# Queueing loads and output transposes behind the next transpose of the row maximum, in an attention and two-layer MoE kernel

## The chip, the cores and the metric

The kernel runs on one core of a Trainium2 chip. The metric is device time of one execution in microseconds. Three executions of the kernel before took 803.95, 791.01 and 797.76 us; the median is 797.76 us.

## The reference, cut to what matters

Sixteen heads (2 batches of 8) of clustered attention, then two pairs of dense layers on the joined heads:

```python
q_n, k_n, c_n = (x / (norm(x) + 1e-6) for x in (q, k, centroids))
mask   = argmax(q_n @ c_n.T) == argmax(k_n @ c_n.T)      # 16 clusters
scores = where(mask, q @ k.T / sqrt(64), -1e9)           # 768 x 768 per head
attn   = exp(scores - max(scores)); attn /= sum(attn) + 1e-9
x      = (attn @ v), heads joined: 1536 x 512
x      = softplus(x @ w_in)  @ w_out                     # 512 -> 2048 -> 512
out    = leaky (x @ w_in2) @ w_out2                      # 512 -> 2048 -> 512
```

The inputs are float32, the weights come as 64-bit floats.

## The kernel before

**Attention, one head at a time.** Everything is kept as pairs of 16-bit halves. For head h, `split` (L188) makes halves of q and k and has them transposed by a DMA (tile `t`, L197). `assign_mm` and `assign_el` (L200 to L234) find the cluster of each row: 24 small matmuls and five VectorE operations, L219 to L225. The one-hot clusters go beside q and k into the tiles `nq` and `nk`, which two more DMA transposes (`tq`, L232; `tk`, L233) turn. `emit_s1` (L239) makes the scores a first time, 12 matmuls of 384 columns (L244), and takes each half row's maximum on VectorE (L251, tile `mm`). `emit_m` (L253) folds them into one maximum per row (L256), writes it into `nq` and has `nq` transposed once more: the tile `tm` (L259). Only then can `emit_s2` (L262) make the scores a second time with the maximum subtracted inside the matmul (L277, and L278, which reads `tm`), ScalarE takes the exponential (L284), GpSimd its low half (L286), and `emit_pv` (L291) multiplies by v (L300, L313, L314, L318). `emit_empty` (L333, matmuls L336) ends the head, `emit_norm` (L338) divides and, after each second head, transposes the joined result into the MoE's input by two DMAs (`xth`, `xtl`, L360). v itself is loaded by `load_v` (L177, DMA L180) two heads ahead and split by `split_v` (L183).

**Weights.** A weight matrix arrives in pieces of 512 KB, 16 per matrix, through two staging tiles `st` (DMA L134). `conv` turns a piece into two half-precision tiles: three integer operations on VectorE (L142, L145, L148), one copy on ScalarE (L152), and one subtraction on VectorE (L153). A staging tile is free again after L148. `w_step` (L516) traces the conversion of the last piece and the load of the next one. Pieces are counted here from 0: 0 to 15 are w_in, 16 to 31 w_out, 32 to 47 the second w_in and 48 to 63 the second w_out. The last 32 go into memory that the attention's tiles hold until its end.

**MoE.** The tokens go in four blocks of 384. `layer_in` has 16 steps of 12 matmuls (L415), each followed by an activation (L383 and L384 on ScalarE, L385 on VectorE; block 0 has another form, L393 to L398); `layer_mid` has 4 outputs of 48 matmuls (L428), which are evacuated by L432 and L433; the second pair is L415 again and `layer_out` (L447, output L453). Steps of block 0 are traced among heads 8 to 15.

**What sets the order.** All DMAs are issued by SyncE (SP), in one order, and an issue that waits holds up all behind it. Every engine executes its instructions in the order that a list scheduler made when the program was built: it takes what is ready by a priority (`at_pri`; a lower number is earlier, a head is one unit) in a timeline of its own. So an edge that is added at one place moves instructions elsewhere too. `tc.issue_after(x)` adds such an edge: what is traced in the block stands behind instruction x on x's own engine. PSUM has eight banks: two rings `s1` and `s2` of two banks for scores, one each for `as` and `x`, and `m0` and `m1` for weights and MoE. In heads 0 to 7 the ring `s2` takes `m1` as a third bank.

## Time and profile before

| | before |
|---|---|
| median of three runs | 797.76 us |
| the profiled execution, its own time | 799.24 us |
| its span, first to last instruction | 797.5 us |
| TensorE busy in the span | 732.4 us, 92% |
| VectorE, ScalarE, GpSimd busy | 389.3, 318.6, 189.2 us |
| mean granted TensorE clock | 0.949 of full speed |
| transposes of the maximum (`tm`), issue to landing | 2.5 to 4.7 us, median 2.8 us, 16 of them |

The page's first part gives busy time by engine, its second the busy tenths of forty equal slices of the span (19.9 us each) with the clock that TensorE was granted. Times are microseconds from the span's start. SP, the queue that issues DMAs, is never counted as busy; its waits are in a view of their own. A busy TensorE can be a slow one: at half clock a matmul takes twice as long and is busy all the while, so busy time is read beside the granted clock.

### The profile page before, as it was taken

The page shows a single profiled execution, that of the slowest core. Times are in us where ns is not written, and L with a number is a line of the kernel's source. Part 1 is how long each engine was busy: PE and PEld are TensorE (multiplying, and loading weights), DVE is VectorE, ACT ScalarE, POOL GpSimd, SP SyncE. Part 2 cuts the span into 40 slices and gives each one's busy share as a digit, 9 for nine tenths or more (in the row PEclk, how much of TensorE's full clock was granted, in tenths as well). Part 3 has the DMA queues.
Part 4 walks back from the last instruction along what each step waited for, and adds up shares of the span by engine and source line. Part 5 has one row for each costly group of instructions (what it writes and reads, how often), then busy time and mean ns, then how long its engine had stood idle before and what let it go on. Part 6 is the DMA issues. An engine that isn't in the chain of part 4 may idle for free.

```text
span 797.5 us, 14209 instructions
## 1 busy us (share of the span) xinstructions
PE 732.4 (92%) x5808; PEld 439.6 (55%) x5808; DVE 389.3 (49%) x819; ACT 318.6 (40%) x739; POOL 189.2 (24%) x176
## 2 busy tenths in 40 slices
PE   1589989889889898899998999999999999999998
PEld 1167757545556565566564566666545645645643
DVE  4876767588798888328788902201201200200210
ACT  5366655537766646135224503303402402411410
POOL 4256655437766747200000000000000000000000
PEclk9988978669899899999999999999999999999999
DMA  8986444684854655214455300000000000000000
GB/s 196 228 173 129 103 106 109 159 156 130 167 143 130 131 105 134 80 21 131 151 168 163 129 1 1 1 1 0 1 14 27 1 14 26 2 14 27 1 14 26
DMA packets 104881, 66.03 MB, mean 83 GB/s; under 512 B 90992, under 2 KB 95088, under 8 KB 104816
## 3 DMA queue, kind: packets, MB, share of 16 engines
q1 hardware_dynamic: 104816, 65.13, 33.5%
q8 instruction: 45, 0.74, 0.4%
q14 instruction: 20, 0.16, 0.1%
HBM read 43.02 MB, written 3.15 MB: 58 GB/s over the span
## 4 chain that ended last, share of the span: by engine, by line
PE 65%; DMA 16%; DVE 12%; ACT 3%; issue 2%; SPq 1%; POOL 0%; ACTq 0%; DVEq 0%
PE m L415 23%; PE m L447 16%; PE m L428 11%; DMA tm<-nq 4%; DMA st<-in_moe_w_in_dram 4%; DMA st<-in_moe_w_out_dram 3%; PE s L278 3%; PE s L244 3%; PE s L277 2%; DMA t<-n 2%; DVE mm L251 2%; PE x L300 2%; DVE wc L148 2%; DVE wc L145 2%; DMA tk<-nk 1%
## 5 line engine op out<-in xcount | busy, mean ns | idle before, releaser
L385 DVE TENSOR_TENSOR g_l<-mr,g_h 128x384 f16<-128x384 f32 x112 | 62.3, 557 | 208.4 <-ACT mr L384 208.4
L286 POOL TENSOR_TENSOR pl<-p 128x768 f16<-128x768 f32 x80 | 117.4, 1474 | 84.2 <-ACT p L284 70.2
L251 DVE TENSOR_REDUCE mm<-s 128x1 f32<-128x384 f32 x192 | 102.4, 552 | 30.7 <-PE s L244 29.7
L415 PE MATMUL m<-xth,w_inh 128*128 128x384 f16 x256 | 86.5, 339 | 4.8 <-DVE xtl L433 3.9
L383 ACT ACTIVATE g_h<-m 128x384 f16<-128x384 f32 x112 | 54.6, 488 | 89.5 <-PE m L415 89.5
L428 PE MATMUL m<-g_h,w_outh 128*128 128x384 f16 x256 | 83.5, 326 | 4.4 <-DVE w_outl L153 2.6
L415 PE MATMUL m<-xtl,w_inh 128*128 128x384 f16 x256 | 86.4, 338 | 0.0
L428 PE MATMUL m<-g_l,w_outh 128*128 128x384 f16 x256 | 83.4, 326 | 2.3 <-DVE g_l L385 2.2
L428 PE MATMUL m<-g_h,w_outl 128*128 128x384 f16 x256 | 83.3, 326 | 0.0
L415 PE MATMUL m<-xth,w_in2h 128*128 128x384 f16 x256 | 83.3, 326 | 0.0
L415 PE MATMUL m<-xtl,w_in2h 128*128 128x384 f16 x256 | 83.3, 326 | 0.0
L284 ACT ACTIVATE p<-s 128x384 f32<-128x384 f32 x144 | 67.4, 492 | 31.1 <-PE s L278 28.6
L244 PE MATMUL s<-tk,tq 80*128 80x384 f16 x192 | 68.7, 381 | 12.1 <-DVE mm L251 7.9
L415 PEld LDWEIGHTS <-w_inh 128*128 128x128 f16 x512 | 51.4, 101 | 41.0 <-issue 10.6
L447 PE MATMUL m<-w_out2h,g_h 128*128 128x512 f16 x192 | 72.8, 379 | 0.0
L447 PE MATMUL m<-w_out2l,g_h 128*128 128x512 f16 x192 | 72.8, 379 | 0.0
L447 PE MATMUL m<-w_out2h,g_l 128*128 128x512 f16 x192 | 72.8, 379 | 0.0
L428 PEld LDWEIGHTS <-w_outh 128*128 128x128 f16 x512 | 49.6, 98 | 37.8 <-issue 3.2
L415 PEld LDWEIGHTS <-w_in2h 128*128 128x128 f16 x512 | 50.1, 98 | 33.4
L278 PE MATMUL s<-tm,tk 81*128 81x384 f16 x160 | 57.2, 374 | 11.9 <-DMA tm<-nq 11.4
L447 PEld LDWEIGHTS <-g_h 128*128 128x128 f16 x384 | 37.6, 98 | 44.9
L277 PE MATMUL s<-t 128*128 128x384 f16 x160 | 57.0, 360 | 5.1 <-ACT p L284 4.2
(108 smaller groups left out, 1224.5 us busy)
## 6 DMA issues: line engine op xcount, KB each, us to landing
st<-in_moe_w_in_dram SPq DMA_DIRECT2D x32, 512.0 KB, 4.2
st<-in_moe_w_out_dram SPq DMA_DIRECT2D x32, 512.0 KB, 3.5
qk<-in_q_dram SPq DMA_DIRECT2D x16, 192.0 KB, 3.2
qk<-in_k_dram SPq DMA_DIRECT2D x16, 192.0 KB, 3.3
v<-in_v_dram SPq DMA_DIRECT2D x16, 192.0 KB, 3.1
out_dram<-ob SPq DMA_DIRECT2D x12, 256.0 KB, 2.0
t<-n SPq DMA_TRANSPOSE x16, 4.1
tq<-nq SPq DMA_TRANSPOSE x16, 4.3
```

The lines of the kernel that those rows point to most:

```text
L145: V.scalar_tensor_tensor(out=c, in0=hi, scalar=-0x40000000, in1=c, op0=ALU.bitwise_and, op1=ALU.bitwise_or)
L244: PE.matmul(out=o, lhsT=t[0:KS1, c, :], rhs=tk[0:KS1, 3 * j:3 * j + 3, :], start=True, stop=True,)
L251: V.reduce_max(out=mms[h % 2][:, c, j:j + 1], in_=bank[:, 0:3 * 128], axis=AX)
L277: PE.matmul(out=o, lhsT=t1[:, kt, 1, :], rhs=t1[:, 3 * j:3 * j + 3, 0, :], start=True, stop=False)
L278: PE.matmul(out=o, lhsT=t2[0:KS2, kt, :], rhs=tqh[0:KS2, 3 * j:3 * j + 3, :], start=False, stop=True)
L284: S.activation(out=p[:, j, :], in_=sp, func=AF.Exp, scale=scale)
L286: G.tensor_tensor(out=pl, in0=p, in1=pb, op=ALU.subtract)
L383: S.activation(out=late["h"][:, m, :], in_=hp, func=func, scale=scale, alpha=alpha)
L385: V.tensor_tensor(out=late["l"][:, m, :], in0=r, in1=late["h"][:, m, :], op=ALU.subtract)
L415: PE.matmul(out=hp, lhsT=w_, rhs=x_, start=(i == 0), stop=(i == len(ops) - 1))
L428: PE.matmul(out=yp, lhsT=w_[:, kk, ms], rhs=g_[:, kk, :], start=(n == 0), stop=(n == 3 * KFF - 1))
L447: PE.matmul(out=op, lhsT=g_[:, kk, rs], rhs=w_[:, kk, :], start=(n == 0), stop=(n == 3 * KFF - 1))
```

## The change

Four edits. The dictionary `tmi` keeps the DMA that issues each head's `tm`, and `behind_tm(h)` puts what is traced in its block behind head h's `tm` in SP's order. Three kinds of DMA get it: the load of v for head h+2 (behind `tm` of head h+1), the weight loads traced in the main loop at head h (behind `tm` of head h+1), and the output transposes of a pair of heads whose second is h (behind `tm` of head h+2; those of the last pair of a batch stay free). The two `w_step` calls that stood before the main loop are gone, so the first weight piece is loaded later. In head 0 every second first-maximum matmul takes its bank from the ring `s2`, so that five banks serve it in place of two.

```diff
-    mark = {}
+    mark, tmi = {}, {}
...
     def emit_s1(h, c):
         t, tk = tp2[h]
         for j in range(2):
-            bank = ring("s1", h)
+            bank = ring("s2" if h == 0 and j else "s1", h)
...
-        nc.sync.dma_start_transpose(out=t, in_=nq.rearrange("p c d -> p (c d)"))
+        tmi[h] = nc.sync.dma_start_transpose(out=t, in_=nq.rearrange("p c d -> p (c d)"))
         tpq[h] = t
...
-            with at_pri(h + 1 if hh < H - 1 else h + 1 - LEAD_NORM):
+            with at_pri(h + 1 if hh < H - 1 else h + 1 - LEAD_NORM), behind_tm(h + 2 if hh < H - 1 else NH):
                 for src, dst in ((xh, xt_h[b]), (xl, xt_l[b])):
                     nc.sync.dma_start_transpose(
...
+    def behind_tm(h):
+        return tc.issue_after(tmi[h].ins) if h in tmi else nullcontext()
...
+    wtie = {"h": -1}
...
             if wq:
-                convs.append(w_piece(*wq.pop(0)))
+                with behind_tm(wtie["h"]):
+                    convs.append(w_piece(*wq.pop(0)))
...
     for h in range(AHEAD):
         chain(h)
-        w_step()
     split_v(0)
     for h in range(NH):
         chain(h + AHEAD)
+        wtie["h"] = h + 1
         with at_pri(h):
             if h + 1 < NH:
                 split_v(h + 1)
             if h + 2 < NH:
-                load_v(h + 2)
+                with behind_tm(h + 1):
+                    load_v(h + 2)
             emit_sv(h)
```

**First place: SP, from head 1's `tk` to head 0's `tm`.** The names: `qk` and `v` are loads of q, k and v, `st` a weight piece, `t` the first transposes of heads 3 and 4, `tq` and `tk` those of head 2. Before:

```order
L233 DMA_TRANSPOSE tk<-nk_93 128x6x128
L174 DMA qk<-in_k_dram 128x384
L180 DMA v_2_100<-in_v_dram 128x6x64
L134 DMA st<-in_moe_w_in_dram 128x1024
L197 DMA_TRANSPOSE t_680<-n_673 128x12x128
L232 DMA_TRANSPOSE tq<-nq_89 128x6x128
L233 DMA_TRANSPOSE tk<-nk_94 128x6x128
L173 DMA qk<-in_q_dram 128x384
L174 DMA qk<-in_k_dram 128x384
L134 DMA st<-in_moe_w_in_dram 128x1024
L197 DMA_TRANSPOSE t_978<-n_971 128x12x128
L259 DMA_TRANSPOSE tm<-nq_87 128x6x128
```

Now:

```order
L233 DMA_TRANSPOSE tk<-nk_93 128x6x128
L197 DMA_TRANSPOSE t_664<-n_657 128x12x128
L173 DMA qk<-in_q_dram 128x384
L174 DMA qk<-in_k_dram 128x384
L197 DMA_TRANSPOSE t_962<-n_955 128x12x128
L232 DMA_TRANSPOSE tq<-nq_89 128x6x128
L233 DMA_TRANSPOSE tk<-nk_94 128x6x128
L259 DMA_TRANSPOSE tm<-nq_87 128x6x128
```

The loads of v and of two weight pieces are gone from ahead of `tm` (a third, that stood between the `tk` of heads 0 and 1, too), and a load of k has moved up past head 1's transposes.

On VectorE, the last operations up to head 0's maximum (L256 on `nq_87`; `wcp` is a weight conversion, `svr` a sum of v, `mm_102` head 1). Before:

```order
L251 TENSOR_REDUCE mm_101<-s_242 128x1
L251 TENSOR_REDUCE mm_101<-s_245 128x1
L153 SCALAR_TENSOR_TENSOR w_inl<-wcp,w_inh 128x512
L251 TENSOR_REDUCE mm_101<-s_248 128x1
L251 TENSOR_REDUCE mm_101<-s_251 128x1
L142 TENSOR_SCALAR wcp<-st 128x512
L219 TENSOR_REDUCE mx<-as 128x12
L251 TENSOR_REDUCE mm_101<-s_254 128x1
L251 TENSOR_REDUCE mm_102<-s_314 128x1
L145 SCALAR_TENSOR_TENSOR wcp<-st,wcp 128x512
L220 TENSOR_TENSOR as<-as,mx 128x192
L256 TENSOR_REDUCE nq_87<-mm_101 128x6
```

Now:

```order
L251 TENSOR_REDUCE mm_101<-s_242 128x1
L225 TENSOR_TENSOR oh<-as,m_395 128x192
L251 TENSOR_REDUCE mm_101<-s_239 128x1
L251 TENSOR_REDUCE mm_101<-s_248 128x1
L251 TENSOR_REDUCE mm_101<-m 128x1
L251 TENSOR_REDUCE mm_101<-s_245 128x1
L330 SCALAR_TENSOR_TENSOR svr<-h_464,sel,as 32x65
L251 TENSOR_REDUCE mm_101<-s_251 128x1
L251 TENSOR_REDUCE mm_102<-s_312 128x1
L256 TENSOR_REDUCE nq_87<-mm_101 128x6
```

No conversion stands among them any more; the first one now comes after head 1's maximum.

**Second place: SP, around head 5's `tm` (the row on `nq_87`).** `xth` and `xtl` are the output transposes of heads 2 and 3; `v_1_99` is head 7's v before, `v_2_100` and `v_0_98` are those of heads 5 and 6 now. Before:

```order
L233 DMA_TRANSPOSE tk<-nk_93 128x6x128
L360 DMA_TRANSPOSE xth_83<-xnh 128x6x128
L360 DMA_TRANSPOSE xtl_85<-xnl 128x6x128
L180 DMA v_1_99<-in_v_dram 128x6x64
L259 DMA_TRANSPOSE tm<-nq_87 128x6x128
L134 DMA st<-in_moe_w_in_dram 128x1024
```

Now:

```order
L180 DMA v_2_100<-in_v_dram 128x6x64
L232 DMA_TRANSPOSE tq<-nq_89 128x6x128
L233 DMA_TRANSPOSE tk<-nk_93 128x6x128
L259 DMA_TRANSPOSE tm<-nq_87 128x6x128
L134 DMA st<-in_moe_w_in_dram 128x1024
L360 DMA_TRANSPOSE xth_83<-xnh 128x6x128
L360 DMA_TRANSPOSE xtl_85<-xnl 128x6x128
L180 DMA v_0_98<-in_v_dram 128x6x64
```

The two output transposes and a load of v went from ahead of `tm` to behind it.

**Third place: SP, around the last `tm` (head 15, on `nq_88`).** Before:

```order
L134 DMA st<-in_moe_w_out_dram 128x1024
L259 DMA_TRANSPOSE tm<-nq_88 128x6x128
L134 DMA st<-in_moe_w_out_dram 128x1024
L134 DMA st<-in_moe_w_in_dram 128x1024 x4
L360 DMA_TRANSPOSE xth_84<-xnh 128x6x128
L360 DMA_TRANSPOSE xtl_86<-xnl 128x6x128
L134 DMA st<-in_moe_w_in_dram 128x1024 x12
```

Now:

```order
L259 DMA_TRANSPOSE tm<-nq_88 128x6x128
L360 DMA_TRANSPOSE xth_84<-xnh 128x6x128
L360 DMA_TRANSPOSE xtl_86<-xnl 128x6x128
L134 DMA st<-in_moe_w_out_dram 128x1024 x5
L360 DMA_TRANSPOSE xth_84<-xnh 128x6x128
L360 DMA_TRANSPOSE xtl_86<-xnl 128x6x128
L134 DMA st<-in_moe_w_in_dram 128x1024 x16
```

Of the 32 pieces of the first weights, 31 were loaded ahead of the last `tm` and 27 are now; none of the second weights is loaded any more before the last output transposes, where four were. On TensorE, which goes with it, head 15's last matmuls (L336) stood behind all four outputs of block 0's `layer_mid` and one step of block 1 and now stand ahead of three of the outputs, of nine matmuls of the first one, and of block 1.

On VectorE, from the last output of block 0's `layer_mid` (L433) on; the L385 after it are the 16 products of block 1. Before, with pieces 32 to 34 of the weights under way:

```order
L433 SCALAR_TENSOR_TENSOR xtl_85<-m,xth_83 128x384 x4
L347 TENSOR_SCALAR x<-x 128x6
L348 RECIPROCAL dd<-x 128x6
L350 TENSOR_TENSOR y<-x,dd 128x384
L385 TENSOR_TENSOR g_l<-mr,g_h 128x384 x3
L153 SCALAR_TENSOR_TENSOR w_in2l<-wc,w_in2h 128x512 x2
L142 TENSOR_SCALAR wc<-st 128x512
L385 TENSOR_TENSOR g_l<-mr,g_h 128x384
```

Now, with pieces 44 to 46:

```order
L433 SCALAR_TENSOR_TENSOR xtl_85<-m,xth_83 128x384
L148 SCALAR_TENSOR_TENSOR wc<-st,wc 128x512
L142 TENSOR_SCALAR wc<-st 128x512
L385 TENSOR_TENSOR g_l<-mr,g_h 128x384
L145 SCALAR_TENSOR_TENSOR wc<-st,wc 128x512
L153 SCALAR_TENSOR_TENSOR w_in2l<-wc,w_in2h 128x512
L148 SCALAR_TENSOR_TENSOR wc<-st,wc 128x512
L385 TENSOR_TENSOR g_l<-mr,g_h 128x384
```

The division of head 15 (L347 to L350) has moved ahead of the outputs, the first product of block 1 from piece 34 to piece 45. The sixteenth, which stood at piece 43, stands at piece 51 now, and the 16 products of block 2, which stood among pieces 55 to 63, behind piece 63.

## Rows read from the trace of the kernel before

**Rows 1.** The view of cores: span and mean granted TensorE clock.

```profile
core 0: 797.5 us, clock 0.949
```

**Rows 2.** By stretch: busy PE, PEld, DVE, ACT, POOL (instructions); clock, DMA share, GB/s.

```profile
107.00:124.00 17.00, 13.96 (x101) 9.25 (x96) 8.56 (x19) 7.28 (x16) 6.68 (x6) 0.57 0.35 89
141.00:155.00 14.00, 11.24 (x96) 8.22 (x97) 7.40 (x16) 7.57 (x18) 6.89 (x7) 0.60 0.79 194
176.00:278.00 102.00, 91.73 (x1047) 59.62 (x1045) 87.35 (x187) 67.03 (x160) 69.32 (x61) 0.90 0.63 143
380.00:460.00 80.00, 73.66 (x439) 43.27 (x437) 66.40 (x121) 30.81 (x65) 0.00 (x0) 0.98 0.48 149
460.00:797.00 337.00, 333.79 (x1866) 182.28 (x1863) 48.55 (x87) 81.68 (x180) 0.00 (x0) 1.00 0.03 10
```

**Rows 3.** Waits of TensorE from 38 to 311: total us, times, longest.

```profile
PE s L278 <- DMA tm<-nq: 10.8, 6, 3.0
```

**Rows 4.** Timeline of SP's issues before head 0's `tm`: start, us, line.

```profile
18.13 0.57 SPq L134 DMA_DIRECT2D st<-in_moe_w_in_dram  x1
...
23.58 1.69 SPq L197 DMA_TRANSPOSE t<-n  x1
25.37 3.07 SPq L232 DMA_TRANSPOSE tq<-nq  x1
28.54 1.36 SPq L233 DMA_TRANSPOSE tk<-nk  x1
...
34.69 1.49 SPq L259 DMA_TRANSPOSE tm<-nq  x1
```

**Rows 5.** Timeline of VectorE, from head 0's first maximum to head 1's last.

```profile
19.99 0.56 DVE L251 TENSOR_REDUCE mm<-s 128x1 f32<-128x384 f32 x1 [0.82 <-PE s L244]
20.47 0.35 DVE L221 TENSOR_TENSOR as<-as,tab 128x192 f32<-128x192 f32 x1
...
31.78 1.02 DVE L251 TENSOR_REDUCE mm<-s 128x1 f32<-128x384 f32 x2
32.72 0.69 DVE L145 SCALAR_TENSOR_TENSOR wcp<-st,wcp 128x512 int32<-128x512 int32 x1
...
33.59 0.18 DVE L256 TENSOR_REDUCE nq<-mm 128x6 f16<-128x18 f32 x1
...
49.75 0.17 DVE L256 TENSOR_REDUCE nq<-mm 128x6 f16<-128x18 f32 x1
```

**Rows 6.** Timelines of SP and TensorE around the `tm` of heads 1, 5, 7.

```profile
49.93 2.50 SPq L197 DMA_TRANSPOSE t<-n  x1
...
104.26 1.24 SPq L360 DMA_TRANSPOSE xtl<-xnl  x1
...
55.31 0.48 PE L278 MATMUL s<-tm,tk 81*128 81x384 f16 x1 [1.77 <-DMA tm<-nq]
...
110.99 0.48 PE L278 MATMUL s<-tm,tk 81*128 81x384 f16 x1 [3.02 <-DMA tm<-nq]
...
144.12 0.48 PE L278 MATMUL s<-tm,tk 81*128 81x384 f16 x1 [1.95 <-DMA tm<-nq]
```

**Rows 7.** The chain of waits, in order of time: start, us, what.

```profile
34.69 3.50 DMA tm<-nq
...
106.26 4.68 DMA tm<-nq
...
350.05 0.30 PE x L336 x6
...
353.28 2.82 DMA xtl<-xnl
...
362.36 5.02 DMA st<-in_moe_w_in_dram
...
446.66 3.48 DMA st<-in_moe_w_out_dram
...
482.27 31.20 PE m L415 x192
```

More of the change, by code (lines that the diff above doesn't have):

```diff
@@ L1 @@
-from contextlib import ExitStack, contextmanager
+from contextlib import ExitStack, contextmanager, nullcontext
 import concourse.bass as bass
```

## Prediction

> **What bounds the kernel now.** I read the mean clock first: 0.949 over the whole span [rows 1], of two levels, 1.2 and 2.4 GHz, so somewhere TensorE ran at half speed for some time; the next view says where. By stretch [rows 2], the last 337 us are all matmul (333.8 of 337 us busy at full clock): nothing in this change shortens them. So the time is decided by when that block begins, and that by the attention (0 to 350 us) and by the second weights' conversion, which follows it (to 457 us). In the attention TensorE is nearly always busy, but not at full clock: 0.57 and 0.60 in two stretches [rows 2]. Of its idle time from 38 to 311 us the largest item by far is `tm`: 10.8 us in six waits [rows 3]. The reader is to see two things in the timelines around these waits [rows 6]: the issue of `tm` stands behind other DMAs in SP's one order, and after such a wait the clock is low: the wait of 3.02 us ends at 110.99 and lies in the stretch at 0.57, the one of 1.95 us ends at 144.12 in the stretch at 0.60 [rows 2, 6]. VectorE is the second engine to watch: 87.35 of 102 us busy in the later heads [rows 2], a good part of it weight conversions.
>
> The profiled execution took 799.24 us in a span of 797.5; the median of the runs is 797.76, 1.5 lower. I sum against the profiled one.
>
> **The change, part by part.** No arithmetic is added or taken away; 64 conversions, 64 weight loads and 16 loads of v stay. Each term is a shift of one landmark.
>
> (a) Head 0's `tm`. It is issued at 34.69 [rows 4], 1.1 us after its maximum began at 33.59 [rows 5]. VectorE now has between 19.99 and that maximum, by the order shown, 13 half-row maxima at 0.51 (a pair takes 1.02), three assignment operations at 0.35, 0.29 for the sum of v (an operation on 32 rows, put below the 0.35) and 0.18: 6.6 + 1.05 + 0.3 + 0.2 = 8.2 us, so the maximum ends at 28.2. The two weight pieces there took six operations of 0.69 = 4.1 us; the rest of the 13.8 us was waits for score banks, which five banks in place of two should cover. On SP, from 18.13: a load 0.57, `tq` and `tk` 1.3 each, `t` 1.7, two loads 0.5 each, `t` 1.7, `tq` and `tk` 1.3 each and 0.1 between issues make 11.1, so 29.2 at the earliest. (`tq` of head 2 took 3.07, the like `tk` 1.36 [rows 4]; with two weight pieces and a load of v fewer in flight I take the short one.) SP is the later: `tm` at 29.2, **-5.5 us**; bounds -4 (`tq` still slow) and -7 (VectorE decides).
>
> (b) Head 1's `tm`. Its maximum began at 49.75, but `tm` waited for the 2.50 us that a `t` took on SP [rows 5, 6], and TensorE idled 1.77 us. The `t` now stands behind. Conversions of 0.69 also leave VectorE's order there. **-3 us** more (2.5 of SP, the rest VectorE); bounds -1 and -5.
>
> (c) Heads 5 and 7. Ahead of head 5's `tm` stood two output transposes and a load of v; from the second transpose at 104.26 to the issue at 106.26 [rows 6, 7] is 2.0 us, and the landing took 4.68 instead of the median 2.8. That is 3.9 us against a wait of 3.02. Head 7 had one output transpose ahead. I take the two waits, 3.02 + 1.95 = **-5 us**. The low clock behind them is worth up to 17 x 0.43 + 14 x 0.40 = 12.9 us if TensorE bounds those stretches and keeps full clock: so the bounds are 0 and -17.9. I stay near the waits, because the heads from 55.31 to 110.99 came at 13.9 us each with the clock mostly up, and those to 144.12 at 16.6: two heads at the faster pace give back 5.3.
>
> (d) Heads 7 to 8. The `tk` of head 8 now stands behind a weight load whose staging tile waits for a conversion, and that for head 6's division, much as before: **0**; bounds -3 and +2.5, one wait for `tm`.
>
> (e) Heads 8 to 15. 18 conversions stand between the maxima of heads 8 and 15 in place of 20, so VectorE has 2 x 4 x 0.69 = 5.5 us less to do in a stretch where it is 86% busy: **-4 us**; bounds 0 and -5.5.
>
> (f) The tail. Before, head 15 ended at 350.05, and block 2's `layer_mid`-outputs were done and block 3's input began at 482.27 [rows 7]: 132.2 us. Now less stands ahead of head 15's end: three outputs of 48 matmuls, nine matmuls, and one input step of 12. At 31.20/192 = 0.1625 us a matmul that is 26.8 us. So head 15 ends at 323.2 less the sum of (a) to (e). After it TensorE has 149.7 us of work to the same landmark (32 input steps of 1.95, 11 outputs of 7.8, nine matmuls). But VectorE's order puts block 1's sixteenth product at weight piece 51. The second weights start when head 15's output transpose has landed, 353.28 + 2.82 - 350.05 = 6.05 us after its end; four of them were loaded beforehand, now the first load, 5.02 [rows 7], comes on top; then 20 pieces at (446.66 - 362.36)/25 = 3.37 us each (loads of pieces 37 and 62). Product 16 comes at 6.05 + 5.02 + 67.4 = 78.5 us after head 15. From there three outputs (23.4), block 2's input (31.2) and its four outputs (31.2): 164.3 us, more than the 149.7 of work. The landmark moves from 482.3 to 323.2 + 164.3 = 487.5: **+5 us**; bounds -9.4 (TensorE never waits) and +13.5 (the last three of the w_out pieces, 8.3 us of VectorE, come on top of the wait for the first load instead of inside it). I take the middle because the 5.02 is long enough to hold most of them.
>
> Sum: -5.5 - 3 - 5 - 4 + 5 = -12.5, so 786.7 for an execution like the profiled one, and 1.5 less, 785, for the median; since three runs spread by 13 us, I put **786**. The bounds together run from -48 to +11.
>
> **Rivals.** *The clock comes back* (22%). If no wait above a microsecond is left in heads 1 to 8, the clock stays up and (c) is worth 10 to 18 us instead of 5. Rows 2 and 6 speak for it (each low stretch begins with such a wait), against it that some waits are for `t` and `tk`, which the change does not move forward. 799.24 - 17.5 to - 30: 767 to 780.
>
> *The tail takes it back* (18%). Weights are loaded later: 27 pieces ahead of the last `tm` instead of 31, and none of the second set early. VectorE's conversions from the end of attention, not TensorE, then set the block that follows; by (f) this decides as soon as product 16 comes later than 64 us after head 15 (149.7 - 85.8). With (f) at its bound of +13.5, only (a) and (b) gained, and one new wait of TensorE at 2.5 us, the time is 799.24 - 8.5 + 13.5 + 2.5 = 807, slower than before; 797 to 810 with other parts. For it: TensorE's work and VectorE's order are within 15 us of each other there already, and VectorE is busy 66.4 of 80 us while the second weights are converted [rows 2]. Against it: the attention ends some 27 us earlier in the program's order, so the conversions start earlier too. The Trainium skill speaks for this rival: its page "DMA: Bandwidth & Descriptors", section "Rules for kernel authors", says to issue a DMA early and wait for it late, so that its fixed setup is hidden. By that rule every load in this change moves the wrong way, and the sum would be this rival's 807 and not 785; the trace of before speaks half against it, since there the early weight loads stand ahead of the `tm` that TensorE waits for.
>
> *Nothing to speak of* (7%). The issues move, but VectorE and TensorE set when a maximum is ready, and only the first 5.5 us come, less the tail's 5: 795 to 800.
>
> **How the numbers follow.** The forecast has 53%, its own range 779 to 795. About 2% is what a measurement of this kernel can tell from no change: 781.8 and 813.7. Faster by more: the clock's rival and a little of the forecast's lower end, 0.26. Slower by more: the top of the tail's rival, which needs another wait as well, 0.05. Within: 0.69. The range for 8 in 10 reaches into both rivals: 769 to 804 leaves out some 6% below and 9% above.
>
> **What would show it.** (a) head 0's `tm` issued at 29 to 30 and landed by 33; (b) head 1's second scores (L278) starting at 46 to 48 instead of 55.3; (c) no wait of L278 for `tm` above 1 us in heads 5 and 7, and the clock above 0.8 from 100 to 140; (e) head 15's `tm` issued near 291 instead of 308.6; (f) head 15's last matmuls (L336) at 304 to 310, block 1's sixteenth product (L385) 75 to 85 us later, and block 3's input 160 to 168 us after head 15. What would make it wrong: new waits for v (L324) right behind head 1's end, since head 2's v is now loaded behind head 1's `tm`; TensorE waiting in the first output of `layer_mid` for w_out's last pieces; a clock that stays low for another reason although `tm` is prompt.

## The result: slightly slower, where 12 us less were forecast

Twenty runs of the changed kernel have a median of 801.82 us (794.78 to 810.99), twenty of the kernel before beside them 796.05; the ratio of the two is 1.007, 95% interval [1.0046, 1.0094]. That is within 2%, but slower, where the forecast of 786 was 1.5% faster. (Ratios here and below leave out runs more than 1.5% above the fastest of their version, as disturbed; medians are of all runs.) The profiled execution of the changed kernel took 801.82 us in a span of 799.8, against 799.24 before.

**Both ends of the forecast's chain came as forecast.** The chain of waits after the change, in order of time (start, us, what), the lines that answer to [rows 7]:

```profile
30.40 2.72 DMA tm<-nq
...
44.93 5.06 DMA st<-in_moe_w_in_dram
...
303.07 2.51 DMA tm<-nq
...
319.19 0.30 PE x L336 x6
...
324.73 4.42 DMA st<-in_moe_w_in_dram
...
422.22 31.20 PE m L415 x192
453.42 31.20 PE m L428 x192
484.62 15.44 PE m L415 x95
```

Head 0's `tm` is issued at 30.40 instead of 34.69. Head 15 ends at 319.2 instead of 350.05, 30.9 earlier, of which 26.8 is work that moved behind it: a gain of 4.1. From there to block 3's input (484.6) it takes 165.4 us; the forecast had 164.3. So the start and the length of the tail are right. Of the 17.5 us that the forecast had gained by head 15's end, 13.4 are missing; they went between head 1 and head 15, whose `tm` comes at 303.07 and not at 291.

**Where the waits of TensorE went.** Its waits from 38 to 311 us (total, times, longest), first before, the row beside [rows 3] that counts here, then after:

```profile
PE s L244 <- DVE mm L251: 2.3, 4, 1.5
```

```profile
PE s L278 <- DMA tm<-nq: 8.4, 6, 2.5
PE s L244 <- DVE mm L251: 7.4, 11, 1.6
PE s L277 <- ACT p L284: 3.5, 10, 1.0
PE as L206 <- DMA t<-n: 3.5, 3, 2.0
PE s L244 <- DMA tk<-nk: 1.5, 2, 1.0
```

The reader is to see that the wait for `tm`, on which the forecast stood, shrank by 2.4 us (10.8 to 8.4), and another, of first scores for a bank that VectorE's half-row maxima (`mm`) free, grew by 5.1. All its waits in that stretch together are 25.1 us before and 29.0 after. A wait that is taken away at one place of such a chain is worth only what the next one leaves.

What ScalarE and VectorE waited for in that stretch after the change; none of these three lines is in the answer for before:

```profile
ACT v L185 <- DMA v<-in_v_dram: 3.0, 3, 1.6
```

```profile
DVE wcp L142 <- DMA st<-in_moe_w_in_dram: 6.3, 3, 2.4
DVE svr L330 <- ACT h L329: 5.1, 4, 2.1
```

Loads that now land late are waited for by instructions in the middle of an engine's order. An example from VectorE's timeline (start, us, instruction, in brackets the idle time before it and its releaser): the first weight load, issued behind head 1's `tm` at 44.93, lands at 49.99, and the maxima stand behind its conversion.

```profile
47.26 0.36 DVE L225 TENSOR_TENSOR oh<-as,m 128x192 f16<-128x192 f32 x1
50.02 0.69 DVE L142 TENSOR_SCALAR wcp<-st 128x512 int32<-128x512 int32 x1 [2.40 <-DMA st<-in_moe_w_in_dram]
50.62 1.01 DVE L251 TENSOR_REDUCE mm<-s 128x1 f32<-128x384 f32 x2
```

By stretch, the rows that answer to [rows 2] (columns as there):

```profile
107.00:124.00 17.00, 15.39 (x107) 10.61 (x107) 9.34 (x20) 7.37 (x18) 6.54 (x6) 0.53 0.34 88
141.00:155.00 14.00, 12.75 (x155) 8.75 (x154) 8.65 (x21) 9.79 (x25) 9.43 (x8) 0.88 0.95 194
176.00:278.00 102.00, 88.75 (x1019) 56.43 (x1016) 80.40 (x177) 62.83 (x150) 66.74 (x58) 0.92 0.67 143
380.00:460.00 80.00, 80.00 (x494) 48.19 (x493) 53.42 (x98) 31.82 (x69) 0.00 (x0) 1.00 0.32 103
```

One of the two low stretches is still there (0.53), the other gone (0.88); the mean over the span is 0.953 (before 0.949).

### The profile page after: what moved, and what is told of

Same layout as the page of the kernel before. It is cut to its first block, busy times and chain, and to the rows that moved or that the text cites. A ratio compares the mean times of both kernels' runs of the same rounds, so it can differ in the third digit from the quotient of the medians.

```text
span 799.8 us, 14210 instructions
## 1 busy us (share of the span) xinstructions
PE 731.6 (91%) x5808; PEld 437.8 (55%) x5808; DVE 388.7 (49%) x819; ACT 319.2 (40%) x739; POOL 188.3 (24%) x176
## 4 chain that ended last, share of the span: by engine, by line
PE 72%; DMA 13%; DVE 7%; ACT 4%; SPq 2%; issue 2%; POOL 1%; ACTq 0%; POOLq 0%; DVEq 0%
PE m L415 30%; PE m L447 16%; PE m L428 12%; DMA st<-in_moe_w_in_dram 5%; PE s L244 3%; DMA tm<-nq 2%; PE s L277 2%; PE s L278 2%; ACT p L284 2%; DMA tk<-nk 2%; DVE mm L251 2%; PE x L300 1%; DMA t<-n 1%; PE x L318 1%; PE x L313 1%
## 5 line engine op out<-in xcount | busy, mean ns | idle before, releaser
L385 DVE TENSOR_TENSOR g_l<-mr,g_h 128x384 f16<-128x384 f32 x112 | 62.2, 558 | 220.5 <-ACT mr L384 220.4
L251 DVE TENSOR_REDUCE mm<-s 128x1 f32<-128x384 f32 x190 | 100.6, 551 | 26.4 <-PE s L244 25.1
L415 PE MATMUL m<-xth,w_inh 128*128 128x384 f16 x256 | 89.0, 348 | 9.8 <-DVE xtl L433 4.3
L415 PE MATMUL m<-xtl,w_inh 128*128 128x384 f16 x256 | 89.0, 348 | 0.2 <-DMA xtl<-xnl 0.2
L244 PE MATMUL s<-tk,tq 80*128 80x384 f16 x190 | 65.3, 371 | 12.0 <-DVE mm L251 8.6
L428 PEld LDWEIGHTS <-w_outh 128*128 128x128 f16 x512 | 49.6, 98 | 37.5 <-issue 3.3
```

Source lines behind the costliest of these rows:

```text
L244: PE.matmul(out=o, lhsT=t[0:KS1, c, :], rhs=tk[0:KS1, 3 * j:3 * j + 3, :], start=True, stop=True,)
L251: V.reduce_max(out=mms[h % 2][:, c, j:j + 1], in_=bank[:, 0:3 * 128], axis=AX)
L385: V.tensor_tensor(out=late["l"][:, m, :], in0=r, in1=late["h"][:, m, :], op=ALU.subtract)
L415: PE.matmul(out=hp, lhsT=w_, rhs=x_, start=(i == 0), stop=(i == len(ops) - 1))
L428: PE.matmul(out=yp, lhsT=w_[:, kk, ms], rhs=g_[:, kk, :], start=(n == 0), stop=(n == 3 * KFF - 1))
```

## The experiments

The change has five parts: the second **ring**, the **later start** of the weights, and three kinds of ties: of the **loads of v**, of the **output transposes**, of the **weight loads**. Eighteen runs of versions with some of them were made. Since a version's runs spread by 0.9 to 2.4%, the table also has each version's mean granted clock and its time at one clock, told below. I go by the median of all runs and by the column at 0.955; the ratio of `no_wtie` rests on two of its six runs. The versions ran on five chips; the kernel before, run beside them on each, had medians of 796.2 to 797.4.

```
version       edits it has, of ring/late start/weight/output/v   median   runs  clock  at 0.955   ratio to before
before        -                                                  796.99   121   0.955   796.9
changed       ring late weight output v                          801.82    20   0.955   802.1   1.007 [1.005, 1.009]
rings         ring                                               796.04    12   0.958   797.5   0.997 [0.994, 1.001]
v_only        v                                                  791.60    12   0.969   800.3   0.995 [0.991, 0.999]
x_only        output                                             805.97     6   0.958   806.9   1.012 [1.007, 1.017]
rvx           ring output v                                      802.10    12   0.954   801.8   1.005 [1.001, 1.008]
rnx           ring late output                                   789.73    12   0.963   794.5   0.993 [0.989, 0.997]
no_wtie       ring late output v                                 799.51     6   0.958   799.2   0.990 [0.983, 0.997]
no_vx         ring late weight                                   794.79    12   0.957   796.0   0.999 [0.995, 1.002]
no_x          ring late weight v                                 806.97     6   0.953   805.8   1.012 [1.008, 1.016]
no_v_n        ring weight output                                 796.10    12   0.961   799.0   0.999 [0.995, 1.003]
early_w       ring weight output v                               804.35    12   0.954   803.3   1.008 [1.003, 1.012]
no_ring       late weight output v                               805.34    12   0.951   802.5   1.009 [1.005, 1.013]
no_v          ring late weight output                            784.57     6   0.967   792.0   0.984 [0.980, 0.988]
no_v_again    the same                                           785.12     6   0.968   792.1   0.985 [0.979, 0.991]
v_early       all five, v tied one head earlier                  799.71    12   0.957   799.4   1.002 [0.997, 1.006]
lag2          all five, conversions a step later                 795.19    12   0.957   796.0   1.001 [0.997, 1.005]
lag2_no_v     no_v, conversions a step later                     785.74     6   0.966   794.1   0.987 [0.982, 0.993]
lag2_no_vx    no_vx, conversions a step later                    798.77    12   0.953   797.3   1.004 [1.001, 1.007]
before_lag2   before, conversions a step later                   789.43     6   0.969   796.7   0.981 [0.977, 0.986]
```

**Time at one clock.** Every run has its mean granted clock. Taken from each version's own mean, the 315 runs scatter about a line of 6.0 us less per 0.01 of mean clock, by 2.1 us (standard deviation). "At 0.955" is a version's mean time moved along that line to a clock of 0.955. I read it as what the order of the work costs in waits, and the rest as clock. The 6.0 agrees with the forecast's price of low clock: 0.01 of 797 us is 15.9 us at half speed, so 0.38 us per us, where the forecast had 0.40 to 0.43.

The traces allow a check that does without the line. Every version has the same 5808 matmuls, so a profiled span is TensorE's busy time, which goes with the clock, plus its idle time. The engines' busy times of the changed kernel, of `no_v` and of `no_v_again`, whose spans are 799.8, 783.7 and 776.8 us:

```profile
PE 731.6 (91%) x5808; PEld 437.8 (55%) x5808; DVE 388.7 (49%) x819; ACT 319.2 (40%) x739; POOL 188.3 (24%) x176
```

```profile
PE 724.1 (92%) x5808; PEld 434.9 (55%) x5808; DVE 387.7 (49%) x819; ACT 319.5 (41%) x739; POOL 188.7 (24%) x176
PE 714.7 (92%) x5808; PEld 429.5 (55%) x5808; DVE 388.5 (50%) x819; ACT 318.9 (41%) x739; POOL 188.7 (24%) x176
```

TensorE is idle for 65.1 us before (797.5 less 732.4), 68.2 in the changed kernel, 59.6 and 62.1 without the ties of v. Over the twenty profiles idle time and the column at 0.955 go together (correlation 0.89), so the column does tell waits in the main, though not to a microsecond.

### First: weights, or all ties? (rings, rvx, no_wtie, lag2)

`rings` and `rvx` leave the weights as before; `no_wtie` and `lag2` are the changed kernel with

```diff
-                with behind_tm(wtie["h"]):                 # no_wtie
-                    convs.append(w_piece(*wq.pop(0)))
+                convs.append(w_piece(*wq.pop(0)))
...
-            if convs:                                      # lag2
+            if len(convs) > (1 if wq else 0):
```

> The kernel before with one part of the change alone: the second bank of head 0's first maxima comes from the other ring. No load is tied to anything and weights begin as before. Theory A (loads that are issued late stall VectorE's conversions, and the maxima behind them, in heads 1 to 4): nothing is late here, so head 0's second scores start 4 to 5 us earlier than before (33 to 34 instead of 38.2) and that gain is still there at head 4 (91 to 92 instead of 96.0); total 790 to 793. Theory B (the early heads are elastic: their pace is set by something the change does not touch, and any head start is used up by head 4, whatever loads are tied): head 0 starts 4 to 5 us earlier, head 4 at 95 to 96; total 795 to 798. Theory C (what was lost is lost in the tail, by weights converted later): by the order 17.6 us less TensorE work stands ahead of head 15's end, and block 1's sixteenth product stands at weight piece 49 instead of 43, so the time from head 15's end to block 3's input is 155 to 160 us, some 8 more than 132.2 + 17.6 = 149.8; total 797 to 800.

Measured: 796.0; head 0's second scores at 35.0, head 4's at 97.1 (before 96.0). The gain is used up by head 1 (second scores at 55.5, before 55.31), earlier than theory B had it; the tail (146.5 us) is not what theory C had.

> The changed kernel with the weights put back: two weight pieces before the first head, weight loads not tied; the two rings, the ties of v and of the output transposes stay. The order has 232.7 us of TensorE work ahead of head 15's end (before: 230.8) and block 1's sixteenth product at piece 42 (before: 43), so its tail is that of before. Theory A (weight loads tied behind the maximum's transpose stall the conversions): no wait of VectorE for a weight load above 1 us in heads 1 to 4, head 4's second scores at 89 to 91, total 787 to 791. Theory B (early heads elastic): head 0 at 33 to 34, head 4 at 95 to 96, total 795 to 797. Theory C (tail): the early gain may stay or go, but from head 15's end to block 3's input it takes 130 to 135 us as before, and the total is 6 us or more under the changed kernel's: 790 to 796.

Measured: 802.1, slower than before with the weights as before. So the weights are not needed for a loss: adding the ties of v and of the output transposes to `rings` cost 6 us. Theories A and C fall as the whole cause (the tail took 131.7 us, as forecast by C, and the version is slow all the same). Theory B missed too: it had head 4's second scores at 95 to 96 and 795 to 797, and they came at 100.5.

> The changed kernel with the ties of the weight loads taken out; weights still begin two pieces later. Theory A: the first weight load is then issued well before 44.93, VectorE's first conversion has its data (wait for the load under 0.5 us instead of 2.40), head 2's second scores start at 61 to 63 instead of 65.3, head 4's at 90 to 92 instead of 95.5; total 795 to 798. Theory B: head 4 at 94.5 to 96 as in both kernels; total 800 to 803. Theory C: the order puts block 1's sixteenth product at piece 49 instead of 52, three pieces of 3.37 us earlier at most, from head 15's end to block 3's input 155 to 160 us with 9.2 us more work ahead of head 15's end; total 796 to 800.

Measured: 799.5 with runs from 786 to 805, too wide to decide between A and B. Head 4's second scores came at 96.2, as in both kernels (B).

> The changed kernel with each weight piece converted one weight step later than its load (the two staging tiles allow it); all ties stay. Theory A: the load has landed when VectorE comes to the conversion; waits of VectorE for weight loads in heads 1 to 4 fall from 6.3 us to under 1 us; head 2's second scores start at 61 to 63 instead of 65.3 and head 4's at 90 to 92 instead of 95.5; total 796 to 799. Theory B: head 4 at 94.5 to 96; total 800 to 804. Theory C: one piece fewer is converted before the tail, block 1's sixteenth product stands at piece 51 instead of 52; tail as in the changed kernel within 3 us, total 799 to 805.

Measured: 795.2, 6.6 less than the changed kernel, as theory A had it; but VectorE's waits for weight loads fell only from 6.3 to 4.8 us, so not by theory A's path, and ScalarE waited 8.6 us for v where the changed kernel has 3.0.

This pair shows something else. Up to the maximum of head 6 the changed kernel and `lag2` have the same instructions in the same order on every engine. Yet head 4's second scores started at 95.5 in the one profile and at 89.5 in the other. By stretch, from head 1's second scores to head 2's, first the changed kernel, then `lag2`:

```profile
46.20:65.30 19.10, 17.26 (x198) 12.94 (x197) 13.24 (x30) 11.59 (x28) 11.18 (x10) 0.73 0.81 188
```

```profile
45.00:60.10 15.10, 13.82 (x196) 10.17 (x196) 12.42 (x28) 10.77 (x26) 10.13 (x9) 0.89 0.86 175
```

The same work, some 197 matmuls, 19.1 us at a clock of 0.73 and 15.1 at 0.89. In both, TensorE's longest wait in the stretch was for `mm`, 1.4 and 1.3 us, some 5 us into it. One execution's clock is partly luck; a loss that one profile shows in heads 1 to 4 is not yet a loss of the version. From here on I compare medians and the column at one clock.

### Second: which tie? (no_v, no_x, before_lag2, lag2_no_vx)

```diff
-                with behind_tm(h + 1):                     # no_v
-                    load_v(h + 2)
+                load_v(h + 2)
...
-            with at_pri(...), behind_tm(h + 2 if hh < H - 1 else NH):      # no_x
+            with at_pri(...):
```

> The changed kernel with the loads of v untied; all else of the change stays. So far: rings alone 796.0 us, rings with the ties of v and of the output transposes 802.1, the changed kernel 801.8. Theory D (what is put behind one transpose in SP's one order stands ahead of the next ones; TensorE's waits move from tm to t and tk): the 16 loads of v are most of it, since they stand in every head; without their ties 796 to 799, TensorE's waits for t and tk from 38 to 320 us together 3 us or less (changed kernel 5.0). Theory E (late weight loads hold up VectorE's conversions, and the maxima behind them; TensorE waits for banks that the maxima free, 7.4 us in the changed kernel, 2.3 before): the weight ties stay, so 800 to 803 and 6 to 8 us of these waits. Theory F (each tie only reshuffles the list scheduler's order, and the differences are chance): anything from 795 to 803, with no wait that follows the tie.

Measured: **784.6**, far better than even theory D had, and better than both kernels. TensorE's waits from 38 to 311 us in it, to be read against those of the changed kernel above:

```profile
PE s L277 <- ACT p L284: 5.7, 10, 2.2
PE as L206 <- DMA t<-n: 5.5, 6, 1.5
PE s L278 <- DMA tm<-nq: 4.2, 8, 1.0
PE m L428 <- ACT w_outh L152: 3.7, 3, 2.0
PE s L244 <- DVE mm L251: 2.2, 5, 0.7
```

`tm` 8.4 to 4.2, none longer than 1.0; `mm` 7.4 to 2.2. The waits for t and tk, on which theory D rested, did not fall but rose (5.0 to 7.5): that theory named the right tie for a wrong reason. Of ScalarE's and VectorE's lines shown above, the one for v is gone, and VectorE waits 3.4 us for a weight load and 0.2 for `h`.

> The changed kernel with the output transposes untied; all else of the change stays. Theory D: the output transposes come every second head only, so with the loads of v still tied 800 to 802; if it is they (1.2 to 2.1 us each on SP, two at a time) that stand ahead of t and tk, 796 to 799. Theory E: 800 to 803, TensorE's waits for banks that the maxima free 6 to 8 us. Theory F: anything from 795 to 803.

Measured: 807.0, worse than any theory had. The ties of the output transposes are a gain of 5 us in the changed kernel (3.7 at one clock). TensorE waited 7.8 us for `tk` (1.5 with them).

> The kernel before, none of the change, but each weight piece converted one weight step later than its load. In the changed kernel that step took 801.8 to 795.2. Theory E: the gain there came from conversions that no longer wait for loads issued late; in the kernel before VectorE waits only 0.6 us for a weight load, so there is nothing to gain: 796 to 799. Rival: the later conversion is good by itself (fewer conversions between the maxima, 14 in place of 15 ahead of head 10's): 789 to 793. Theory F: anything from 792 to 802.

Measured: 789.4, in the range of the rival and not in theory E's; its six runs go from 779 to 797. At one clock it is 796.7, the same as before's 796.9: by that column what it gained is clock. The waits that theory E spoke of were not there to mend, and yet the version is faster.

> The changed kernel with conversions one step later, and with the loads of v and the output transposes untied: rings, later start and tied weight loads remain. Theories D and E together: both losses are mended, 788 to 792. Theory E alone (the ties of v and output transposes cost nothing once the conversions are later): 794 to 797. Theory F: 794 to 800.

Measured: 798.8 (797.3 at one clock). Losses do not add up as D and E wanted. The later conversion helps only with v tied (`lag2`, by 6.0 at one clock); with v free it costs 1.3 and 2.1 there (`lag2_no_vx` against `no_vx`, `lag2_no_v` against `no_v`).

### Third: late, or in the wrong place? (v_early, v_only, no_vx, lag2_no_v)

```diff
-                with behind_tm(h + 1):                     # v_early
+                with behind_tm(h):
```

> The changed kernel with all its ties, but each load of v tied behind the transpose of the maximum one head earlier (head 2's v behind head 0's, and so on; the three buffers of v allow it). So far: changed kernel 801.8, without the ties of v 784.6. Theory G (v arrives too late: ScalarE's copy of v waits for the load, 3.0 us in the changed kernel and nothing before or without the ties, and what stands behind it in ScalarE's, GpSimd's and VectorE's orders waits too): v is a head earlier here though still queued behind a transpose, so 784 to 790, ScalarE's waits for v 0.5 us or less, TensorE's waits for banks that the maxima free 2 to 4 us instead of 7.4. Theory D (what counts is that the load stands directly behind the transpose, where it is in flight with it and ahead of t and tk): the same crowd behind each transpose, 798 to 803. Theory F (reshuffled order, chance): 785 to 803 with no relation to these waits.

Measured: 799.7, in theory D's range and not in theory G's. Tying v a head earlier gives back 2.7 of 10 us at one clock. But ScalarE still waited 4.3 us for v, so v was not in time here either: the run shows that this does not mend the loss, and not that a late v is harmless.

> The kernel before with the ties of v alone; one ring, weights and output transposes as before. Theory G: ScalarE waits 2 to 8 us for v from 28 to 320 us (before: none), and the kernel is slower than before: 800 to 804. Theory D: the same, and TensorE's waits for t and tk rise from 4.7 us to 8 or more. Theory F: 794 to 802, no wait for v that matters.

Measured: 791.6, slightly faster than before (0.995), which only theory F's wide range came near. At one clock it is 3.4 us slower, ScalarE waits 8.0 us for v, TensorE's waits for t and tk rise from 4.7 to 9.6: the waits came as G and D had them, and a mean clock of 0.969 instead of 0.955 outweighs them.

> The changed kernel with neither the loads of v nor the output transposes tied: two rings, later start and tied weight loads. Taking out the ties of the output transposes alone made the changed kernel 5 us slower (807.0), taking out those of v alone 17 us faster (784.6). If the two add: 787 to 793. If the ties of the output transposes matter only where v is late as well (both then reach SP between the same transposes): 783 to 787. Theory F: 793 to 800, as with the later conversions (798.8).

Measured: 794.8. With v free, the ties of the output transposes are again a gain (794.8 to 784.6; 4.0 us at one clock). The time is in theory F's range and above the 787 to 793 of parts that add.

> The changed kernel without the ties of v and with each weight piece converted one weight step later. Theories E and G together (both waits mended, the gains of 6.6 and 17 us add, less what both count): 777 to 783. Theory G alone (once v is early VectorE has slack and the conversions' waits cost nothing): 783 to 787. Theory F: 786 to 800.

Measured: 785.7 (794.1 at one clock): with v free, the later conversion adds nothing.

### Fourth: do the parts add? (x_only, rnx, no_v_n, no_v_again, early_w, no_ring)

Each is the kernel with the parts that the table lists; the two early weight steps are

```diff
     for h in range(AHEAD):
         chain(h)
+        w_step()                                           # no_v_n, early_w
```

> The kernel before with the ties of the output transposes alone. Theory H (the ties' effects on the waits add, and the clock comes on top): at a mean clock of 0.955 4 us less than before's 796.6, so 791 to 794; at its own clock of 0.950 to 0.968 a median between 785 and 797. Theory F (the effects do not add, each order is its own case): at 0.955 outside 790 to 795.

Measured: 806.0, the slowest but one. Theory H falls: the same ties that gain 3 to 4 us at one clock beside the later start (three pairs: `no_vx` and `no_v`, `no_x` and changed, `lag2_no_vx` and `lag2_no_v`) cost 10 alone. Alone they also lack the ring and the weights' ties.

> Two rings, weights begun later but untied, output transposes tied, loads of v untied. Theory H: rings and weights cost or gain 1 to 2 us, the output transposes' ties gain 4: at a mean clock of 0.955 791 to 795, and 5 us or more under the same version with v tied (no_wtie, 799.2). Theory F: 796 or more, no better than with v tied.

Measured: 789.7, 794.5 at one clock, in H's range, and 4.7 under `no_wtie` there, where H had 5 or more.

> The changed kernel without the ties of v and with the two early weight steps put back: rings, weight ties and ties of the output transposes. Theory H: at a mean clock of 0.955 790 to 795, within 3 us of the version without ties of v (791.9). If the later start of the weights is what made room early on (head 0's and head 1's transposes 5 and 8 us earlier), 795 to 799. Theory F: anything.

Measured: 796.1, 799.0 at one clock, 7.0 more than `no_v`, from which it differs in the later start alone: that start is what makes the room. TensorE's waits for `t` go with it, all from 38 to 311 us: 9.6 in `x_only`, 9.8 in `no_v_n`, 9.5 in `early_w` and 8.2 in `rvx`, the four versions with output transposes tied and early weight steps; in the nine with those ties and the later start 2.3 to 6.5. One of each, `no_v_n` and then `no_v_again`:

```profile
PE as L206 <- DMA t<-n: 9.8, 6, 3.6
```

```profile
PE as L206 <- DMA t<-n: 3.1, 5, 0.9
```

> The version without the ties of v once more, on another run of the chip. If its clock belongs to its order: mean clock 0.963 to 0.970 and a median of 782 to 788. If the clock belongs to the chip and the moment: mean clock 0.953 to 0.960, median 789 to 794. At a mean clock of 0.955 791 to 793 either way.

Measured: 785.1 at 0.968. Time and clock came again within 0.6 us and 0.001, on another chip: by this one repeat a good mean clock belongs to the order, though single executions of it still run from 778.65 to 790.42.

> The changed kernel with the two early weight steps put back, all ties and the rings kept. If the later start of the weights makes the room that the ties of v and of the output transposes need: TensorE's waits for t rise from 3.5 to 8 us or more, 806 to 810 at a mean clock of 0.955 (changed kernel 802.1). If the early steps are worth having, because four pieces more are converted before the tail: 797 to 800. If neither: 801 to 803. Ties of v cost 3.7 us at that clock alone and 10 in the changed kernel; against the version without them and with early steps (799.1) the same 4 to 10 give 803 to 809.

Measured: 804.4 (803.3 at one clock) and 9.5 us for `t`: the wait of the first of the three cases, but a smaller price than its 806 to 810; against the changed kernel 1.2 us at one clock.

> The changed kernel with one ring for head 0's first maxima; all ties and the later start kept. The forecast put head 0's gain of 5 us down to the rings and to the two weight pieces that no longer stand ahead. If the rings carry it: head 0's second scores at 36 to 38 instead of 33.2, and at a mean clock of 0.955 804 to 807. If the weights carry it: head 0 at 33 to 35, 801 to 803.

Measured: 805.3 (802.5 at one clock); head 0's second scores at 35.3 instead of 33.2. That lies between the two cases. The ring without the later start gave 35.0 (`rings`), but with all ties 37.5 (`early_w`): these single profiles do not settle which of the two carries head 0's gain. At one clock the ring is worth 0.4 us in the changed kernel, nothing clear.

**What the ties of v cost, six times.** Each pair differs in them alone:

```
without ties of v -> with          median              at 0.955       waits for mm
before     -> v_only            797.0 -> 791.6      796.9 -> 800.3     2.3 -> 5.0
rnx        -> no_wtie           789.7 -> 799.5      794.5 -> 799.2     2.5 -> 3.5
no_vx      -> no_x              794.8 -> 807.0      796.0 -> 805.8     4.3 -> 4.7
no_v_n     -> early_w           796.1 -> 804.4      799.0 -> 803.3     1.7 -> 2.3
lag2_no_v  -> lag2              785.7 -> 795.2      794.1 -> 796.0     3.2 -> 3.9
no_v       -> changed           784.6 -> 801.8      792.0 -> 802.1     2.2 -> 7.4
```

At one clock they cost in all six, 1.9 to 10.1 us; by the median in five, 8 to 17 (the 9.8 of `no_wtie` is the weakest, since its runs spread from 786 to 805). TensorE's idle time in the profiled execution rises in all six too, by 0.8 to 14.0 us. The wait of first scores for the maxima (last column, TensorE, 38 to 311 us) rises in all six, in four of them by 1 us or less in one profile each. In the changed kernel they cost 17 us, which the line splits into 10 of waits and 7 of clock; its profile has 8.6 and 6.1 us more idle time than the two without them.

## Why the prediction was wrong

Heads 0 and 1, (a) and (b): right where they look. Second scores at 33.16 and 46.21 instead of 38.2 (the landing of `tm`, 34.69 + 3.50 [rows 7]) and 55.31 [rows 6], 5.1 and 9.1 us earlier; the terms were 5.5 and 8.5.

Heads 1 to 4: no term, and 8.6 us lost. From head 1's second scores to head 4's, and on to head 8's, before (columns as in [rows 2]):

```profile
55.30:96.00 40.70, 39.73 (x525) 30.07 (x525) 28.22 (x67) 26.05 (x67) 25.07 (x21) 0.84 0.58 109
96.00:170.00 74.00, 63.72 (x702) 44.36 (x702) 50.52 (x114) 39.03 (x97) 37.97 (x33) 0.75 0.56 125
```

and after:

```profile
46.20:95.50 49.30, 44.71 (x562) 32.24 (x561) 37.83 (x87) 29.28 (x72) 27.42 (x23) 0.83 0.65 140
95.50:165.30 69.80, 60.90 (x720) 42.53 (x719) 47.84 (x113) 38.33 (x98) 37.42 (x33) 0.81 0.60 132
```

In the first of these stretches VectorE has 16 conversion operations (L142, L145, L148, L153) where it had 3, some 9 us more at 0.69 each: (a) and (b) counted that they leave heads 0 and 1 and charged nothing where they come back. No run moves them alone, so their price is argued. `lag2`, with the same instructions in the same order, took 44.5 us there, `no_v`, with the same 16 operations, 44.4: so some 4 of the 8.6 us come again in both, with the ties of v and without, and the rest is not shown to be more than this one execution.

Heads 4 to 8, (c) and (d): 69.8 us where before 74.0, so 4.2 less for a forecast of 5. Head 7 no longer waits for its `tm` (1.95 before), and its low stretch is gone. But head 5 still waits 2.51 us, and head 3, outside the stretch, now waits 1.96:

```profile
108.61 0.80 PE L278 MATMUL s<-tm,tk 81*128 81x384 f16 x2 [2.51 <-DMA tm<-nq]
```

Heads 7 to 8 by themselves, (d), priced at nothing: from second scores to second scores 24.4 us (140.9 to 165.3) where before 25.9 (144.1 to 170.0), inside its bounds.

Heads 8 to 15, (e): failed. From head 8's second scores to head 15's end 153.9 us, where before 180.0 less the 26.8 of work that moved made 153.2: nothing gained for a forecast of 4.

The tail, (f): right in size. 165.4 - 26.8 = 138.6 us where before 132.2, +6.4 for a forecast of +5. Its path is off: the sixteenth product came 73.7 us after head 15 where 78.5 was forecast, and the rest took 91.7 instead of 85.8, so the agreement is partly luck. The rival of the tail gave the right sign, but not by its mechanism: head by head the loss lies ahead of the tail. Its rule of the Trainium skill ("DMA: Bandwidth & Descriptors", "Rules for kernel authors": issue early, wait late) agrees with the ties of v, and the weights speak against it: started later, 796.1 became 784.6 (`no_v_n`, `no_v`).

**The step that failed.** Head 15's `tm` is issued at 303.07, 12 us later than the 291 that (a) to (e) gave. The step is the one that has no term: "16 loads of v stay". The forecast charged what the move takes away ahead of `tm` and put v's new place under what would make it wrong, without a price. The runs put that price at 17 us by the median (801.8 against 784.6), 10 at one clock. The sign that the forecast had named for it, a wait for v (L324), is there only once, 1.2 us; the loss came by other waits. Without the ties of v most landmarks come. In `no_v` the chain reads

```profile
287.21 2.48 DMA tm<-nq
...
459.93 8.61 PE m L428 x53
468.54 21.61 PE m L415 x133
```

with head 15's `tm` at 287.2 (forecast 291), its end at 302.6 (304 to 310), block 3's input 165.9 us later (160 to 168), no wait for `tm` above 1.0 us, and a median of 784.6 and 785.1 for a forecast of 786.

That the number is met so closely is partly luck. The forecast's sum of 12.5 us was waits and work, with next to no clock in it; of the 12.4 us that `no_v` has on before, 7.5 are its clock (0.967) by the line, and 4.9 its waits. TensorE's waits from 38 to 311 us did not even shrink in all (25.1 before, 25.8 in `no_v`): those for `tm` fell from 10.8 to 4.2, as (c) had it, and others grew. Heads 1 to 4 lost 3.7 us there as well, and heads 4 to 8 gained 9.5 instead of 5. The part of (c) that rests on the output transposes was seen beside the later start only: alone their ties cost 10 us at one clock.

The clock's rival came half true, by these 7.5 us. But the clock did not follow from fewer waits, as that rival had it: `v_only` waits more than before and has 0.969.

**Open.** By which path the ties of v cost what they cost is not settled, nor that it is by VectorE's maxima. Tying v a head earlier gives back 2.7 of 10 (`v_early`), though v still came late there; VectorE's wait for weight loads alone is not it (`lag2`). The place is open too: against `no_v` the changed kernel loses 4.9 us in heads 1 to 4, 5.3 in heads 4 to 8, 7.4 from there to head 15's end and nothing in the tail, but `lag2` against `lag2_no_v` gains 1.0, loses 11.0 and gains 4.1 in the same three stretches. That the ties act only through the list scheduler's order, theory F, is not excluded. And what in an order makes its mean clock 0.95 or 0.97 none of the runs tells; only that it came again with the order in one repeat.

## What to carry to other kernels

Price each kind of transfer that an edit queues behind another by itself, also the one that seems to be just moved along: here four parts of the change gained 12 us and the fifth cost 17 (5 and 10 at one clock). Work that leaves one stretch must be charged in the stretch where it comes back. A wait that ends last in a profile gives its length only if nobody else in the chain becomes late; after the edit, add up the waits of the engine by releaser, not the one that was aimed at. Where runs of one version spread by more than the effect, split time into clock and waits before reading any single profile: at one clock, versions could be told apart to two microseconds or so, and idle time in the profiles is a check on it. The version to keep is the change without the ties of v.

## What was not expected of the hardware

Mean granted clock differs between orders of the same work, 0.951 to 0.969 over these versions, worth 11 us at 6.0 us per 0.01. It came again with the order on another chip (0.967 and 0.968 without the ties of v), and the kernel before had means of 0.953 to 0.957 on five chips. Between executions of one order it still spreads: `no_v_again` had 0.959 to 0.976 in six runs, with times from 790.42 down to 778.65. The same 197 matmuls or so, with a wait of 1.4 or 1.3 us among them, ran once at 0.73 and once at 0.89.
